# Spectral layer with a mixture of experts on one core: four scatters in flight for the last pair, other PSUM banks for the early jobs, and a new written order

## The chip, the cores and the metric

One core of a Trainium2 chip runs the whole kernel in one launch. The metric is the device time of one execution in microseconds; lower is better. The numbers of an execution differ a little between runs, so the time of a kernel is the median of several.

## The reference, cut to what matters

```python
X  = np.fft.rfft(x, axis=1)                      # x: 8 batches, 1856 positions, 256 channels, float32
Yr = Xr @ w_r - Xi @ w_i + b_r                   # the spectrum goes through a complex 256 x 256 layer
Yi = Xr @ w_i + Xi @ w_r + b_i
Yr = sign(Yr) * max(|Yr| - 0.01, 0)              # soft threshold, the same for Yi
y  = np.fft.irfft(Yr + 1j * Yi, n=1856, axis=1)  # back to 14,848 rows of 256 channels
# routing: one of 4 groups by argmax(y @ w_group), then one of the group's 4 experts; weight = product of both softmax values
h  = max(y[rows of an expert] @ w1[g, e], 0)     # 256 -> 1024
out[rows] = weight * (h @ w2[g, e])              # 1024 -> 256
```

## The kernel before, in words

The eight batches go through in four *pairs*. The transform of 1856 = 29 x 64 positions is made of matmuls. Most products are split into a high and a low part, and three matmuls are added up for one product.

Until about 550 us the kernel follows a written order, the string `ORDER` (lines 58 to 78). Each of its 2040 letters issues one step on one engine, and every engine works through its own steps in that order and never passes over one that waits. Within one letter the steps come by number, so "the 17th s" is the first s of the second pair. These are the letters that matter here.

- TensorE (PE): `c` first transform stage (`a_mm`, line 622), `e` second stage (`f_mm`, 636), `k` the complex layer (`m_mm`, 679, 24 matmuls), `r` first inverse stage (`b_mm`; line 326 for three pairs, 715 for the last), `v` second inverse stage (326), `x` a transpose (`p_turn`, 750), `G` the gate logits (773), `U` and `D` the two matmul layers of an early job (`up_mm` 845, `down_mm` 866 and 867).
- VectorE (DVE): `d` (352), `h` (654), `o` the threshold's sum (692), `q` and `u` low parts (594), `s` the transpose that brings an `r` result into the row tile `v` (`b_turn`, 719), `R` one small step of the routing (185 to 268), `V` low part of an expert's weights (`w_low`, 807), `I`, `T`, `Y`, `B`, `J` steps of an early job (297, 455, 834, 855, 878).
- ScalarE (ACT): `w` (742), `W` high part of an expert's weights (`w_high`, 802), `X` (830), `A` (851), `E` (873), and others.
- SyncE (SP): `l` loads 1 MB (lines 611 for inputs of pairs 2 and 3, 616 for expert weights), `F` fetches the rows of an early job (445 and 452).
- GpSimd (POOL): `S` scatters 128 rows of one pair to the lists of their experts in DRAM (line 277), `K` stores results (543).

A pair has 32 scatters, numbered over all pairs, so S1 is the first of pair 0, S33 of pair 1, S65 of pair 2 and S97 of pair 3. A scatter waits until the one two places ahead of it has landed (`FLY = 2`). Two sets of row tiles `v` are used in turn halves: the first `s` of pair 1 (s17) overwrites rows that S1 to S16 send, the first of pair 2 (s33) rows that S33 to S48 send, and the first of pair 3 (s49) rows that S65 to S80 send. The framework makes each such `s` wait until those scatters have landed.

Four experts have *early jobs* in the ordered phase, two each of 256 rows. A job fetches its rows (`F`), transposes and splits them (`T X Y`), multiplies (`U`), applies the ReLU in two parts (`A B`), multiplies again (`D`), scales (`E J`) and stores (`K`). After the ordered phase comes a late phase that works through the rest of the lists from about 553 us to the end; its code is written out separately and reads the same lists.

[...] `r` of the last pair writes into `pp`, which `U` uses too. `D` writes into `py` for the first two jobs and into `bank()` for the rest.

Of the kernel before, what the change touches and what calls it, by code (L numbers as in the profile page):

```python
# [58 lines left out]
ljeljjcfedghcfgheidikkfnhgimojknZmojenZmcfoeghZjcdfiehgdikkfnhmgojeinkmfoghZZjiknmojZenmcfoeghZjcdfeghikdiknmf  # L59
ojhgeZnmcfoegdjchZikdikfnhmgojeinkmfoghjZZiknmojZenmcfoejdgcfhghcidZkidknmjoZcnmcdjocdpcdpcdppqdZrZqepsrfqehpg  # L60
rsfiehpgskiqqqqemfrghrprsipespsnrjkspqqqrmqorfgsrpkhpspisnjqemqfqrghrprsipesnrjsksqqorfomrhgskinsjotuctmuvtdvw
uctwuvtdvtuwcwuvtdtvuwctuwcutldcfdgxnhxjzeydxuiGyoxxyeyGxvykwtuGmxvfznhkwojtguiemxfvnzhgkjwotiuGmxfHvRyRvwhRvw
RRRtvRRwRxRwxtRxRtezRzyGRRnRGRRugjxReRyRRuivRvwkwuoRmvfRkRwRghnRjRRixmRxzeSfzgGRhnxojSeoyciGSdcHcRlRSdRcRRRRcR
RSRkRRdRRSRRRRRRcmRRdSfklRgnhSjdiRdmeoSfRcRgnRcRjSRcRhkRSRdiddScomfkldgShniojSemnkfSoghjiSemnkfSoghppqSpqemqrp
riSsprpsepSsnkfqghjSqiqjrmoSrsprnspeSspkfogjhSqiqrmqSrsprnsepSspkfogSjhqiqrSfqgrhmsriSnespkspjSqpqqSrfqgrhmsri
SnesrjsescotcdtuctuvtukuwtdudxofvgzhvmwvwixwxzteznuxtoGyuvtGwuvtxjuwkztuxfvgzhmkwintojuxfGgzvhmvwiewxnxtzeoyjG
utvHvwRRvuRwRRvtRwRRRxwRxyuxyGRRyvRtGRRwRRuxtxRyRukyRRRRRvmRGfRgkwRRnRRjRRhSvomxweiSzfxghncziSoeljdGcHSRcRdRcR
RRSRcRRRklRRSdRRRRRRRScRRmRRfkghSndidjcSdmocfdghRSendiRcjRSRclRRcRSdkRRddSocmcSfdghnkldjSoiemSnkfojShgiemSnkfo
# [1181 lines left out]
```

## Time and profile before

| What | Value |
| --- | --- |
| median of 3 runs | 1205.69 us (1204.61 to 1211.43) |
| the profiled execution's own time | 1195.48 us |
| its span in the trace | 1193.6 us |
| mean granted TensorE clock of it | 0.989 of full speed |
| busy: PE, DVE, ACT, POOL | 1149.6, 791.7, 672.9, 261.9 us |

The profiled execution is 10.2 us shorter than the median of the runs, and 1.9 us of its time lie outside the span. Durations below come from that one execution. An engine's idle time is given beside the instruction that ended it, with what released it. Matmuls are pipelined: the start of one to the start of the next tells more than the length of one.

### The profile page before, as it was taken

Reading aid. Unit: us, or ns where it says so; the run is one execution under the profiler, and the core shown is the slowest. Engines: PE = TensorE matmul, PEld = TensorE weight load, DVE = VectorE, ACT = ScalarE, POOL = GpSimd, SP = SyncE. Lnnn points to the kernel's source line nnn. Section 1 sums busy time; section 2 is a strip of 40 time slices with the busy share of each in tenths; the row PEclk is TensorE's granted clock in tenths of the full one; section 3 lists DMA queues with packets and bytes.
Section 4 is the critical chain, followed back from the end, with each engine's and each line's share of the span. In section 5 each row is a group of like instructions: output and inputs, shape, how many; then the busy total and the mean of one; then the engine's idle time right before and its main releaser. Section 6 shows DMA issues by size and latency. Waiting matters only on the chain. (4 is left out here: it accounts for less than half of the span.)

```text
span 1193.6 us, 20882 instructions
## 1 busy us (share of the span) xinstructions
PE 1149.6 (96%) x7428; PEld 990.6 (83%) x7428; DVE 791.7 (66%) x1806; ACT 672.9 (56%) x1506; POOL 261.9 (22%) x257
## 2 busy tenths in 40 slices
PE   8999999999999889998899999999999999999997
PEld 5988889897889569887889888888898898798776
DVE  4449676978787778845785845846767566475542
ACT  2777867685778565534364734634546455454432
POOL 1000013503533532561112111111111111111101
PEclk9999999999999999999999999999999999999989
DMA  9872114103311255443353554454434356455200
GB/s 387 327 279 85 37 34 139 66 1 118 118 38 38 66 135 136 142 145 95 96 177 120 150 202 133 120 230 130 121 113 135 110 174 195 118 177 195 102 10 28
DMA packets 114602, 155.82 MB, mean 131 GB/s; under 512 B 89274, under 2 KB 90045, under 8 KB 104000
## 3 DMA queue, kind: packets, MB, share of 16 engines
q1 hardware_dynamic: 95616, 104.33, 28.7%
q0 software_dynamic: 12048, 30.67, 6.9%
q10 hardware_dynamic: 6832, 19.47, 4.2%
q8 instruction: 59, 0.97, 0.3%
q14 instruction: 47, 0.39, 0.1%
HBM read 104.47 MB, written 52.46 MB: 131 GB/s over the span
## 5 line engine op out<-in xcount | busy, mean ns | idle before, releaser
L556 PE MATMUL py<-big,hh 128*128 128x512 f32 x824 | 289.6, 394 | 0.0
L487 PE MATMUL ph<-xth,big 128*128 128x384 f32 (+1 forms) x896 | 255.5, 361 | 4.0 <-ACT xth L474 3.4
L543 POOL DMA_INDIRECT out_dram<-yo,si x123 | 119.8, 974 | 568.7 <-DVE yo L564 497.2
L557 PE MATMUL py<-big,hl 128*128 128x256 f32 x824 | 230.4, 280 | 2.5 <-DVE hl L493 2.3
L277 POOL DMA_INDIRECT xs_d<-v,sloti x128 | 138.7, 1084 | 338.9 <-ACT xh L649 154.6
L493 DVE SCALAR_TENSOR_TENSOR hl<-ph,hh 128x256 fp32r<-128x256 f32 x448 | 151.7, 380 | 62.0 <-ACT hh L491 59.7
L487 PEld LDWEIGHTS ph<-xth,big 128*128 128x128 f32 x896 | 165.7, 189 | 22.5 <-ACT xth L474 6.2
L556 PEld LDWEIGHTS py<-big,hh 128*128 128x128 f32 x824 | 154.5, 187 | 35.8 <-issue 3.2
L491 ACT ACTIVATE hh<-ph 128x256 fp32r<-128x256 f32 x448 | 133.9, 352 | 78.3 <-PE ph L487 74.7
L487 PE MATMUL ph<-xtl,big 128*128 128x384 f32 (+1 forms) x448 | 162.2, 362 | 2.6 <-DVE xtl L475 2.6
L557 PEld LDWEIGHTS py<-big,hl 128*128 128x128 f32 x824 | 155.5, 189 | 4.0 <-DVE hl L493 2.9
L563 ACT ACTIVATE yo<-py,si 128x256 f32<-128x256 f32 x103 | 48.8, 473 | 151.5 <-PE py L557 146.8
L564 DVE SCALAR_TENSOR_TENSOR yo<-py,si,yo 128x256 f32<-128x256 f32 x103 | 49.5, 482 | 109.5 <-ACT yo L563 108.2
L679 PE MATMUL pw<-wh,xh 128*128 128x256 f32 x480 | 120.2, 292 | 0.0
L432 DVE TENSOR_TENSOR big<-xt,big 128x512 fp32r<-128x512 f32 x168 | 114.1, 682 | 0.0
L679 PE MATMUL pw<-wl,xh 128*128 128x256 f32 x480 | 113.5, 278 | 0.0
L431 ACT CAST big<-xt 128x512 fp32r<-128x512 f32 x168 | 103.7, 621 | 0.0
L487 PEld LDWEIGHTS ph<-xtl,big 128*128 128x128 f32 x448 | 84.6, 189 | 12.8 <-DVE xtl L475 5.3
L679 PEld LDWEIGHTS pw<-wh,xh 128*128 128x128 f32 x480 | 90.8, 189 | 2.8 <-issue 2.4
L679 PEld LDWEIGHTS pw<-wl,xh 128*128 128x128 f32 x480 | 90.7, 189 | 2.6 <-issue 2.4
L692 DVE TENSOR_TENSOR big<-rp,rn 128x512 f32<-128x512 f32 x60 | 42.0, 705 | 45.1 <-ACT rp L686 34.2
L636 PEld LDWEIGHTS pg<-CF,big 128*128 128x128 f32 x480 | 63.8, 198 | 8.5 <-issue 2.7
(200 smaller groups left out, 2034.5 us busy)
## 6 DMA issues: line engine op xcount, KB each, us to landing
xt<-in_w_dram SPq DMA_DIRECT2D x50, 1024.0 KB
xs_d<-zero ACTq DMA_DIRECT2D x16, 1170.0 KB
big<-in_w_dram SPq DMA_DIRECT2D x16, 1024.0 KB
xt<-in_x_dram SPq DMA_DIRECT2D x8, 1024.0 KB
xg<-xs_d SPq DMA_DIRECT2D x64, 96.0 KB
xg<-xs_d SPq DMA_DIRECT2D x48, 128.0 KB
big<-in_x_dram SPq DMA_DIRECT2D x4, 1024.0 KB
v<-in_x_dram SPq DMA_DIRECT2D x4, 1024.0 KB
```

The costliest lines, as they stand in the source:

```text
L277: ins = nc.gpsimd.indirect_dma_start(out=xs_d, out_offset=bass.IndirectOffsetOnAxis(ap=sl_, axis=0), in_=row, in_offset=None, bounds_check ...
L431: nc.scalar.copy(out=wt[:, 2 * i, cs], in_=raws[i][:, cs])
L432: nc.vector.tensor_tensor(out=wt[:, 2 * i + 1, cs], in0=raws[i][:, cs], in1=wt[:, 2 * i, cs].bitcast(F32), op=ALU.subtract)
L487: nc.tensor.matmul(o[:, :n], lhsT=a_[:, ch, fs], rhs=b_[:, ch, 0:n], start=k == 0, stop=k == 5)
L491: nc.scalar.activation(out=hh[:, f, :m], in_=ov, func=AF.Relu)
L493: nc.vector.scalar_tensor_tensor(out=hl[:, f, :m], in0=ov, scalar=0.0, in1=hh[:, f, :m].bitcast(F32), op0=ALU.max, op1=ALU.subtract)
L543: ins = nc.gpsimd.indirect_dma_start(out=out, out_offset=bass.IndirectOffsetOnAxis(ap=ids.si[:, t:t + 1], axis=0), in_=ysb, in_offset=None ...
L556: nc.tensor.matmul(o, lhsT=hh[:, f, ts], rhs=w2b[:, :, f, :], start=f == 0, stop=f == 7, skip_group_check=True)
L557: nc.tensor.matmul(o[:, 0:D], lhsT=hl[:, f, ts], rhs=w2h[:, f, :], start=False, stop=f == 7, skip_group_check=True)
L564: nc.vector.scalar_tensor_tensor(out=ysb, in0=o[:, 0:D], scalar=gate_w, in1=ysb, op0=ALU.mult, op1=ALU.add)
L636: nc.tensor.matmul(o[:, m * 128:(m + 1) * 128], lhsT=zys[pr][:, k, ch * 128:(ch + 1) * 128, bt], rhs=T_v[:, k, :], start=True, stop=True)
L679: nc.tensor.matmul(y[:, bt * D:(bt + 1) * D], lhsT=a_[:, bt * 2 + ch, cs], rhs=w_[:, ri, ch, :], start=False, stop=fin, skip_group_check=True)
```

## The change: what it does

The number of scatters in flight becomes a tuple by pair, two for the first three pairs and four for the last. `r` of the last pair writes into `bank()` instead of `pp`. `D` of all jobs writes into `pg`. `py` goes, and `pp` has three banks, so that eight are in use as before. The result tiles `yp` are five instead of three, the fetch buffers `xg` and `xi` five instead of six. Two small filler tiles shift where a few tiles lie in SBUF.

The order is new from end to end. It has the same number of each letter, except that eight copies go from `z` (DVE) to `y` (ACT). Two of its lines, with the old ones they replace, stand in the diff for all.

```diff
-FLY = 2
+FLY = (2, 2, 2, 4)
...
-XI = {6: 4, 2: 8}
+XI = {5: 4, 2: 8}
...
-jShppqpqeSpqrfqripsSrpqrgqgmeSsnkspjSspqrqSfhrgsirmSsrnsepjSspkpqpqSqrqfhrSpsripqrpqSgeqpskSqssSrfhrgsirSsrses
...
+ocHRcRRdScRRRRdcSRRkdlRSRdRcSmfcdghcRnSdikjdSoRRRRRRRkSmRRfRgShnjoRRmcRSiRncldkjSdoRRSRRcmRSncdjocpdlpSdpqepqS
+qrqfgrhprpqSiepqskSfhgiqsSrnsrSpsrpqrmpqSsjkpqSqsrsnSrpsrpSqrmqpsjepSqfeqgShrfiseghprSiqksSssrSfogrsnSrhkmsWis
...
-            if len(sent) >= FLY:
-                tc.add_manual_dep(ins.ins, sent[-FLY], landed, reason="few scatters are on their way at a time")
+            if len(sent) >= FLY[pr]:
+                tc.add_manual_dep(ins.ins, sent[-FLY[pr]], landed, reason="few scatters are on their way at a time")
...
-            for before in range(1, FLY):
+            for before in range(1, min(FLY[pr], len(sent))):
...
     def h_pair(pool, nf):
+        if pool not in shifted:
+            pool.tile([128, 16], F32, name="aside", bufs=1)
...
-            psum["b", pr, j] = o = early["pp"].tile([128, 512], F32, name="ph")
+            psum["b", pr, j] = o = bank()
...
-        xgs[n] = load_rows(early["mp"], slice(e * CAP + j * LEV, e * CAP + j * LEV + LEV), LEV, 6)
+        xgs[n] = load_rows(early["mp"], slice(e * CAP + j * LEV, e * CAP + j * LEV + LEV), LEV, 5)
...
-        apart(early["mp"], 16)
...
-            psum["d", n, t] = early["py"].tile([128, 512], F32, name="py") if n < 2 else bank()
+            psum["d", n, t] = pg.tile([128, 512], F32, name="pg")
...
-                yp.append(ph.enter_context(tc.tile_pool(name="yp", bufs=3)))
+                apart(early["mp"], 8)
+                yp.append(ph.enter_context(tc.tile_pool(name="yp", bufs=5)))
...
-                early["pp"] = ph.enter_context(tc.tile_pool(name="pp", bufs=2, space=PSUM))
-                early["py"] = ph.enter_context(tc.tile_pool(name="py", bufs=1, space=PSUM))
+                early["pp"] = ph.enter_context(tc.tile_pool(name="pp", bufs=3, space=PSUM))
```

Line numbers of the changed kernel are up to two higher than those of before (`b_turn` is line 721 there, `w_low` 809).

The first place is SP's queue around the first row fetches. `L616` (`L618` after) loads 1 MB of expert weights, `L445` and `L452` fetch the ids `xi` and the rows `xg` of one job. Before:

```order
11 L611 DMA xt<-in_x_dram 128x2048 x8
12 L616 DMA xt<-in_w_dram 128x2048 x2
13 L445 DMA xi<-xs_d 128x2x2
14 L452 DMA xg<-xs_d 32x8x64 x4
15 L616 DMA xt<-in_w_dram 128x2048
16 L445 DMA xi<-xs_d 128x2x2
17 L452 DMA xg<-xs_d 32x8x64
18 L616 DMA xt<-in_w_dram 128x2048
19 L452 DMA xg<-xs_d 32x8x64 x3
```

After:

```order
11 L613 DMA xt<-in_x_dram 128x2048 x8
12 L618 DMA xt<-in_w_dram 128x2048 x4
13 L445 DMA xi<-xs_d 128x2x2
14 L452 DMA xg<-xs_d 32x8x64 x4
15 L445 DMA xi<-xs_d 128x2x2
16 L452 DMA xg<-xs_d 32x8x64 x4
```

The third and fourth weight load stand ahead of the first fetch now, and no weight load stands among the first fetches.

The second place is PE's queue at the first inverse stage of the last pair, `r49` to `r64` (`L715`, `L717` after), and the first job's first layer `U` (`L845`, `L846` after). Before:

```order
1676 L679 MATMUL pw<-wh,xl 128x256 x8
1677 L715 MATMUL ph<-big,CI 128x512 x16
1678 L845 MATMUL ph<-xth,big 128x256
1679 L845 MATMUL ph<-xtl,big 128x256
1680 L845 MATMUL ph<-xth,big 128x256 x2
```

After:

```order
1666 L681 MATMUL pw<-wh,xl 128x256 x8
1667 L717 MATMUL bank<-big,CI 128x512 x7
1668 L846 MATMUL ph<-xth,big 128x256
1669 L846 MATMUL ph<-xtl,big 128x256
1670 L846 MATMUL ph<-xth,big 128x256 x2
1671 L846 MATMUL ph<-xtl,big 128x256
1672 L846 MATMUL ph<-xth,big 128x256 x2
1673 L846 MATMUL ph<-xtl,big 128x256
1674 L846 MATMUL ph<-xth,big 128x256 x2
1675 L846 MATMUL ph<-xtl,big 128x256
1676 L846 MATMUL ph<-xth,big 128x256
1677 L717 MATMUL bank<-big,CI 128x512 x9
```

One `U` of the first job stands after seven of the sixteen `r`, and the `r` write into `bank` tiles.

The third place is DVE's queue ahead of s33, the first transpose of pair 2 (`L719`, `L721` after). `L268` ends a routing, `L692` (`L694`) is the threshold's sum, `L654` (`L656`) a low part of the second stage, `L594` (`L596`) the low part that the `r` needs. Before:

```order
294 L268 TENSOR_TENSOR base<-base,inc 128x16
295 L352 STREAM_TRANSPOSE big<-bank 128x16x16x2 x2
296 L692 TENSOR_TENSOR big<-rp,rn 128x512
297 L352 STREAM_TRANSPOSE big<-bank 128x16x16x2
298 L654 TENSOR_TENSOR xl<-pg,xh 128x4x128
299 L352 STREAM_TRANSPOSE big<-bank 128x16x16x2
300 L692 TENSOR_TENSOR big<-rp,rn 128x512 x2
301 L654 TENSOR_TENSOR xl<-pg,xh 128x4x128
302 L692 TENSOR_TENSOR big<-rp,rn 128x512
303 L654 TENSOR_TENSOR xl<-pg,xh 128x4x128
304 L594 TENSOR_TENSOR sl<-big,sh 128x512 x4
305 L719 STREAM_TRANSPOSE v<-bank 128x16x32
```

After:

```order
276 L268 TENSOR_TENSOR base<-base,inc 128x16
277 L352 STREAM_TRANSPOSE big<-bank 128x16x16x2
278 L694 TENSOR_TENSOR big<-rp,rn 128x512
279 L352 STREAM_TRANSPOSE big<-bank 128x16x16x2 x2
280 L596 TENSOR_TENSOR sl<-big,sh 128x512 x4
281 L656 TENSOR_TENSOR xl<-pg,xh 128x4x128
282 L596 TENSOR_TENSOR sl<-big,sh 128x512 x2
283 L721 STREAM_TRANSPOSE v<-bank 128x16x32
```

The transpose stands nearer to the routing: one threshold step instead of four and one `L656` instead of three are left between them. In the string, the stretch from S33 to s33 holds six `k`, six `e`, two `r`, two `x`, one `v` and one `G` of PE's large steps before, and four `k`, four `e`, three `r`, three `x` and two `G` after; thirteen `c` and four `l` stand in it in both. From S1 to s17 three `l` stand before, and none after. From S65 to s49 there is no `l` in either.

## Rows read from the trace of the kernel before

**Rows 1.** The page's span and busy times, with their share of the span and the number of instructions.

```profile
span 1193.6 us, 20882 instructions
...
PE   1149.6 (96%) x7428; PEld 990.6 (83%) x7428; DVE 791.7 (66%) x1806; ACT 672.9 (56%) x1506; POOL 261.9 (22%) x257
```

**Rows 2.** The view by windows: the window's start and end, its length, then the busy time of each engine in it (with the number of instructions), the granted TensorE clock, the share of the DMA engines and GB/s.

```profile
0.00:100.00 100.00, 96.64 (x637) 78.55 (x638) 51.30 (x81) 59.20 (x112) 3.31 (x6) 1.00 0.81 321
...
200.00:210.00 10.00, 9.19 (x69) 8.51 (x67) 5.92 (x8) 7.63 (x15) 5.18 (x6) 1.00 0.18 63
210.00:220.00 10.00, 8.96 (x47) 7.88 (x48) 9.58 (x15) 6.76 (x14) 6.81 (x5) 0.83 0.17 61
...
310.00:320.00 10.00, 8.67 (x63) 7.86 (x62) 8.55 (x13) 8.20 (x17) 5.96 (x6) 1.00 0.20 72
...
440.00:450.00 10.00, 6.93 (x52) 5.79 (x52) 6.34 (x15) 6.69 (x13) 0.00 (x0) 0.83 0.85 180
...
490.00:500.00 10.00, 8.35 (x64) 7.61 (x63) 8.55 (x26) 3.42 (x7) 5.02 (x6) 1.00 0.58 190
...
530.00:540.00 10.00, 5.90 (x43) 5.27 (x44) 3.23 (x5) 2.77 (x5) 6.08 (x7) 1.00 0.24 87
```

**Rows 3.** The timeline of POOL, DVE and PE around s17: start, length, engine, line, operation, tiles, and in brackets the idle time before it and what ended it. S1 starts at 170.78 and S16 at 203.81.

```profile
170.78 1.12 POOL L277 DMA_INDIRECT xs_d<-v,sloti  x1 [149.79 <-ACT xh L649]
...
187.47 1.14 POOL L277 DMA_INDIRECT xs_d<-v,sloti  x1 [3.52 <-DMA xs_d<-v,sloti]
...
203.81 0.97 POOL L277 DMA_INDIRECT xs_d<-v,sloti  x1 [0.30 <-issue]
...
207.29 2.05 DVE L719 STREAM_TRANSPOSE v<-bank 128x512 f32<-128x512 f32 x2 [4.04 <-DMA xs_d<-v,sloti]
...
210.81 0.50 PE L326 MATMUL bank<-sl,tph 128*128 128x512 f32 x1 [1.62 <-DVE sl L594]
```

**Rows 4.** The timeline of POOL and DVE from S33 (276.98) and S48 (312.06) to s33, and SP's weight loads of that stretch.

```profile
276.98 1.40 POOL L277 DMA_INDIRECT xs_d<-v,sloti  x1 [40.05 <-DVE xl L654]
...
288.39 0.97 POOL L277 DMA_INDIRECT xs_d<-v,sloti  x1 [5.19 <-DMA xs_d<-v,sloti]
...
312.06 1.10 POOL L277 DMA_INDIRECT xs_d<-v,sloti  x1 [0.30 <-issue]
...
314.77 1.09 DVE L719 STREAM_TRANSPOSE v<-bank 128x512 f32<-128x512 f32 x1 [1.25 <-PE bank L326]
...
280.14 5.54 SPq L611 DMA_DIRECT2D xt<-in_x_dram  x2
295.43 6.50 SPq L616 DMA_DIRECT2D xt<-in_w_dram  x2
```

**Rows 5.** The timeline of POOL where no load is under way: two scatters of the last pair, with one scatter between them that is not shown.

```profile
411.90 0.97 POOL L277 DMA_INDIRECT xs_d<-v,sloti  x1 [1.04 <-DMA xs_d<-v,sloti]
...
415.10 1.08 POOL L277 DMA_INDIRECT xs_d<-v,sloti  x1 [0.95 <-DMA xs_d<-v,sloti]
```

**Rows 6.** The timeline of PE: one `e` (line 636, to the next start) and one `k` (line 679, from its first matmul to the next step's).

```profile
293.33 1.11 PE L636 MATMUL pg<-CF,big 128*128 128x128 f32 x8
294.27 0.27 PE L247 MATMUL bank<-oh,ones 128*128 128x256 bf16 x1
...
296.56 0.68 PE L679 MATMUL pw<-wh,xh 128*128 128x256 f32 x1
...
299.70 0.59 PE L622 MATMUL bank<-xt,cA 128*128 128x512 f32 x1
```

**Rows 7.** The timeline of PE and DVE in the last pair's first inverse stage.

```profile
411.54 2.04 PE L715 MATMUL ph<-big,CI 128*128 128x512 f32 x4 [0.37 <-DVE v L719]
413.96 2.03 PE L715 MATMUL ph<-big,CI 128*128 128x512 f32 x4 [0.39 <-DVE v L719]
...
423.66 0.35 PE L845 MATMUL ph<-xth,big 128*128 128x256 f32 x1 [0.43 <-issue]
...
414.64 0.69 DVE L807 TENSOR_TENSOR big<-xt,big 128x512 fp32r<-128x512 f32 x1
415.24 1.99 DVE L719 STREAM_TRANSPOSE v<-ph 128x512 f32<-128x512 f32 x2
```

**Rows 8.** The timeline of SP, ACT, DVE and PE around 440 us.

```profile
436.56 1.50 SPq L616 DMA_DIRECT2D xt<-in_w_dram  x1
...
443.10 0.62 ACT L802 CAST big<-xt 128x512 fp32r<-128x512 f32 x1 [3.91 <-DMA xt<-in_w_dram]
...
444.54 0.17 DVE L297 TENSOR_SCALAR si<-xi 128x2 int32<-128x2 f32 x1 [3.66 <-DMA xi<-xs_d]
...
444.78 1.44 PE L750 MATMUL bank<-K,v 128*128 128x128 f32 x6 [2.95 <-ACT v L742]
```

**Rows 9.** The timeline of PE and ACT at the end of the ordered phase.

```profile
531.41 0.38 PE L845 MATMUL ph<-xth,big 128*128 128x256 f32 x1 [1.50 <-DVE hl L855]
538.68 0.39 PE L845 MATMUL ph<-xth,big 128*128 128x256 f32 x1 [2.61 <-issue]
...
529.33 0.62 ACT L830 CAST xth<-sl 128x512 fp32r<-128x512 f32 x1 [5.29 <-PE bank L867]
...
537.30 0.60 ACT L851 ACTIVATE hh<-ph 128x512 fp32r<-128x512 f32 x1 [3.18 <-PE bank L866]
...
553.71 0.44 PE L487 MATMUL ph<-xth,big 128*128 128x384 f32 x1 [2.80 <-ACT xth L474]
```

More of the change, by code (lines that the diff above doesn't have):

```diff
@@ L58 @@
 ORDER = """
[L59 to L68, printed above, removed]
@@ L74 @@
[L74 to L77 removed]
+jlcjljcdcdcdcdcdedcfehgdcfcidgedchcidedkknfghmjeoncfcidgmhkZjdioZenkfghmjoieZnfkghmjoieZnfkghmjoieZfmkhnijogZe
@@ new lines @@
+fmkhnijogZkfmhniojemncfocjdcggdZkZdhiemnkfojZhgienkmfjoZhgienkmfjoZhgienkmfjoZhgienkmfjohgZienemfjkohgZZpiqpqp
+rfrqnhrgisemskpjqpspqprqqfrnrhgsmeijsrpespqkpqpqqsrforhgrnisemsrpjqkpspqpqrqfrsghkpiqssrforhnrisemscgjscdctdct
+otcndldctdmcdjcdeldkoouuucnucfdcmhgicdjdcldcdcdcdvldvwovwxwxeyyxtvyuGwvtxwkuyttutuxuvnfzGvwhtixwkuytmugjoxvnze
+fwhvmixjoGykwttuguxvfyGnhviHewRRwRxmRRxRRvyRRyGRwvRjRxRowkRRRyRRtRRRtRRtGgfeunuRvumRkhgwiRRjRRRRvRfvSowhewSixx
+nykymSgjoSGfenhxmSixzjkzSogeSfGnShkmHiRRjRoSgRRRRReRfSRknRRhmRjRoSgRieRRRSfRRRknRRmhgjSoieSfRpRhpkqpSqpqgiSqne
@@ new lines @@
+RfRRkgRnRmRRhmSjojrofSrsprpqrpqSsgepiSsrnskmpjsSqqSqrfghrsprpSqepqriSsnkpsmsSjqrSfqghrsprpeSspisrSksqqSqrfhSgr
+sirskSshStioutctuvdtvwuutcwuvtvdnwuvwovwxwxyxyxyGyxnGyxetyuctfGugvdthetwuviutxmeuwzjxovtykuwtnumxmojGjvzHfvgov
+wRwRkhwttutuxiuRxfvyRhyGwRvRRiRgRvwReRwRvRnReRRRnwRxRRRkRmRyjomjoGRfRxgRnkRyRmRjRRSRxhxmoyeSzixfGgyhcnSedijlSG
+ocHRcRRdScRRRRdcSRRkdlRSRdRcSmfcdghcRnSdikjdSoRRRRRRRkSmRRfRgShnjoRRmcRSiRncldkjSdoRRSRRcmRSncdjocpdlpSdpqepqS
+qrqfgrhprpqSiepqskSfhgiqsSrnsrSpsrpqrmpqSsjkpqSqsrsnSrpsrpSqrmqpsjepSqfeqgShrfiseghprSiqksSssrSfogrsnSrhkmsWis
@@ new lines @@
+jWoWtkotututunvunVvwVtvVwvwutxwvzWxuwWxVvyzlWVewGVtfxxtuhyeizGfuxghgvykiwttutuxWGWuzvmVvVmwelowxmoxyeyGfnhvjov
+iwkHwRRjRjRRRgRtRRxxfRyRkRhyRmRRRRiRnRRRGgRomkRnjottuRvtumuReRwnRxRfeRyRvgRfRhGgShwviioxSweztxjuejuySvGwSvxwky
+SSxmkznSfoghSjiGefgHRSkmRRhnRRRiSRRjRReRfRgSkoRhmRRiSRRnRRRRRkjRSfghmSonRioRkmRSnRRRRSRRomnSoFSrsrSsrSsrITrsrS
+XYrSsUsrsSABrSsrsrsSrsSrsrsSrsrSsUsWWVtSUAVtuSBUttuvAuAvuwSvBwBSvwtxwxDuttzuvtuvyuFwGwvtFvwuDwITtFDtuXtuvYWFTv
+WwtuDwVFtuvVWxwuUFtVWzWxVAlxWVUByVyGAUlIIIIEIEBFUJAKJBxKAxXzDByYGuxxUyyIGAxxBUyHyRGRRARvRRRRvwRtRDwRRRuxxERRRR
@@ L78 @@
+DyRRyRRGRRDJBRvKWTRWUwRRWxRWRAURWRRBWSWvAzVDwSXBGWVxSEVJvySYDwVSlVxEUVJySVGAVSUlHBSRUARTRBSURRRRRSRDRXRSRRYDAR
+ARSBUBSERRRRJUARSRBUARRSBUSTRDTKXTRKYDRRKRURERRRDSJDASABSDEBAJUSWBWVWVUSWVASVWUBWWSVWVDXSVYDEVSJUSAABDSBUESAJS
+UBABSUSDXSYDKUEJKDKDAAKBDBAKEBUJKUABUDDEJKDAABDBEJDKDEJDKEJK
 """
```

8 lines of the change are left out of this document (removed).

## The prediction

> **What bounds the kernel now.** I read the page's busy times first: TensorE (PE) is busy for 1149.6 of 1193.6 us [rows 1], 44 us short of the span, so nothing the change does on another engine counts unless it ends a wait of PE. The number of PE's steps doesn't change. The second view is the one by windows, to find where PE is idle or slow [rows 2]. In the first 100 us it lacks 3.4 us, from 200 to 220 us 0.81 + 1.04 us, from 310 to 320 us 1.33 us, from 440 to 450 us 3.07 us, from 490 to 500 us 1.65 us and from 530 to 540 us 4.10 us. In two of these windows the granted clock is 0.83, so the work that is done there is slower too. The third view is the timeline of each place: who ended the wait. It names four causes.
>
> At s17, VectorE (DVE) waits 4.04 us until the sixteen first scatters have landed, and PE then waits 1.62 us for DVE [rows 3]. Around 440 us ScalarE (ACT) waits 3.91 us for a weight load that was issued at 436.56 and used at 443.10, behind it stands the copy that PE waits 2.95 us for, and DVE waits 3.66 us for a row fetch of the same queue [rows 8]. In the last pair's first inverse stage PE waits 0.37 to 0.39 us for DVE in every two steps `r` [rows 7]. At the end of the ordered phase PE waits 1.50 and 2.61 us for hidden layers of the early jobs [rows 9].
>
> The step from the ordered to the late phase, where PE waits 2.80 us for the first rows [rows 9], ends in the same letters before and after (`EJK`), so I leave it as it is.
>
> **The change part by part.** The sum is made against the profiled execution's own 1195.48 us. That execution is 10.2 us below the median of the runs shown, so I add the sum to 1205.7.
>
> *Start.* The first steps `c` of the second pair move ahead of `e`, where PE has something to do while DVE finishes. All of the window's loss is 3.4 us [rows 2], most of it before the first data. Two input loads are issued nearer to their use, about 6 us of PE work; the load of rows 8 took 6.5 us from issue to use, so up to 1 us could be lost. Ends -2 and +1, I take **-1**.
>
> *s17.* Sixteen scatters took from 170.78 to about 207.3, 36.5 us [rows 3]. Where no load is under way, two scatters take 411.90 to 415.10, 3.2 us [rows 5], so that sixteen take 8 x 3.2 = 26 us and some 2 us to land. The rest are waits like the 3.52 us before 187.47, beside input loads. The new order has no load between S1 and s17, and the stretch is about as long as before less 3 us, so the scatters are in time. What goes is 1.85 us of idle PE and the lower clock of 210 to 220 us, 0.17 x 8.96 = 1.5 us. Ends 0 (they are late for another reason) and -4, I take **-3.4**.
>
> *s33.* Here the change goes the other way. S33 started at 276.98 and s33 at 314.77, 37.8 us later [rows 4]. The row names PE as the one that ended the last 1.25 us, but S48 left at 312.06 and needs about as long to land, so both came together: the stretch fitted the scatters just about. It was long because four 1 MB loads lie in it. The first two are issued from 280.14 on, the pair of scatters beside them holds up the next until 288.39, 5.19 us of waiting [rows 4]. Against 26 + 2 us undisturbed, each load costs (37.8 - 28) / 4 = 2.5 us. The new order keeps the four loads and takes two `k` and two `e` out of the stretch. A `k` is 299.70 - 296.56 = 3.1 us and an `e` 294.27 - 293.33 = 0.94 us [rows 6], together 8.1 us. An `r`, an `x` and a `G` come in and a `v` goes out; none is longer than an `e` and a half, which I take as 1.5 us. So s33 stands 6.6 us earlier and waits 1.25 + 6.6, some 8 us, for the scatters. All `s` of pair 2 and their low parts queue behind it on DVE, and PE needs them: its next `r` lacks a bank. One `k` (3.1 us) stands in front of that and hides a part. Left are 5 us; a granted clock of 0.83 over 10 us, as after s17, would add 1.5. Ends 0 and +9.5, I take **+5**.
>
> The rows show the pair beside a load ending with the load. [...]
>
> *s49.* No load lies between S65 and s49, before or after. The new stretch is some 3.6 us of PE steps shorter, about 26 us, and sixteen undisturbed scatters take 26 to 28 [rows 5]. Ends 0 and +2, I take **+0.7**.
>
> *First inverse stage of the last pair.* It is bound by DVE: four matmuls follow four after 413.96 - 411.54 = 2.42 us, in which DVE does two `s` and one other step, while PE has 2.04 us of matmuls [rows 7]. The `V` (0.6 us each, 415.24 - 414.64) of the first weights are done earlier in the new order, and a `U` goes in between, which came at 423.66. Five `V` are 3 us of DVE; part comes back in the forward phase of that pair, where DVE and PE have about the same to do. The three banks for `r` instead of two change nothing as long as DVE is the slower. Ends -4 and 0, I take **-2**.
>
> *Around 440 us.* All four weight loads of the first two experts now stand ahead of the first row fetch in SP's queue, and the waits of rows 8 go with their cause: 3.07 us of idle PE and 0.17 x 6.93 = 1.2 us of clock, 4.3 us [rows 2]. Next late is the second row fetch: it reads rows of the second list part, so SP holds all later fetches until S96 has landed. That was 3.66 us of DVE in the row; here I take 1 us of PE. Ends -4.3 and +1, I take **-3.3**.
>
> *Early jobs.* 1.65 + 4.10 us are idle in the two late windows [rows 2]. The ACT steps at 529.33 and 537.30 waited 5.29 and 3.18 us and name matmuls of `D` as what ended it, though by the code neither needs a `D`, but a `U` [rows 9]. I can't say what held them. The new order leaves more steps between a `U`, its `A` and `B`, and the `D` that needs them; three banks of `pp`, two of `pg` and five result tiles give `U` and `D` room. A wait of 4 us on ACT would then be half hidden. `D` in `pg` competes with nothing there, because `e` is done by then. Ends -5.7 and 0, I take **-4**.
>
> *Four in flight.* The last scatters land before the last job is done, before as after, so their end bounds nothing. Four scatters may hold up a row fetch that passes them. I cost it at 0, ends -1 and +1. The tiles moved in SBUF and the eight copies from DVE to ACT (0.6 us each, hidden where neither is the bound) are 0 too.
>
> The sum: -1 - 3.4 + 5 + 0.7 - 2 - 3.3 - 4 = -8.0 us, so 1195.5 would become 1187.5 and the median 1205.7 becomes **1197.7 us**.
>
> **The rivals.**
>
> *No net gain, about 1205.* The late answers of ACT at the end of the ordered phase come from no step of the order, so they turn up again at other steps, and s33 costs its full 8 us: -3.4 + 8 + 0.7 - 2 - 3.3 = 0, so 1205.7. For it: the total work of PE, ACT and DVE is the same, so a new order can only win waits, and these are 15.4 us of idle PE in the windows of rows 2, and 2.7 of clock. Against it: two of the named waits lose their cause, whatever becomes of the rest.
>
> *Slower, about 1213.* One mechanism: the scatters of pair 1 beside the four loads. s33 waits 8 us, DVE falls behind in the stretch that it bounds, the one `k` doesn't hide any, since it was needed for DVE's own input, and the clock stays at 0.83 for 20 us (3 us): +11. What the other places win must then shrink to 4 us, of the 14 forecast, as it would if the fetches held by S96 bring back the wait at 440 us and the job waits recur. +11 - 4 = +7, 1213. It decides from a wait of about 8 us at s33 on. For it: the load count in the stretch is the same and its length isn't. Against it: in the rows each of the stretch's loads was issued when a tile came free, so that a later one may slip behind s33.
>
> *A larger gain, about 1189.* The scatters at s33 land in time because one or two of the loads slip, so the 5 us fall away, and the start and the jobs give all they have: -2 - 3.4 - 3 - 3.3 - 5 = -17.
>
> *The change does not do what it says.* Four in flight do nothing for the end, as reckoned above; that is part of the forecast, not another time.
>
> **How the numbers follow.** The forecast (1193 to 1202) has 45%, no net gain (1201 to 1210) 30%, slower 15%, the larger gain 10%. A measurement of this kernel can tell about 0.5%, 6 us, from no change, so faster means below 1199.7 and slower above 1211.7. Faster: 0.8 of the forecast and all of the larger gain, 46%. Slower: the slower case and the upper edge of no net gain, 17%. The rest, 37%, is the same. For 8 in 10 the range takes in most of the larger gain and the start of the slower case, 1188 to 1212; the forecast's own is 1193 to 1202.
>
> **What would show it.** In the changed kernel's profile, no DVE wait above 1 us at the first `s` of pair 1 and a granted clock of 1.00 after it; a DVE wait of 5 to 8 us for a scatter at the first `s` of pair 2, and PE short by 3 to 6 us there; no wait of ACT for a weight load after the first row fetches; less than 3 us of idle PE in the last 30 us before the late phase. The forecast is wrong if s33 is in time (then too high), or if the job waits come back as long as before (then too low). The late phase must be as long as before within 1 us; if it isn't, the time comes from something that I have not seen.

## The result, and the profile after

The changed kernel takes 1214.93 us (median of 9 runs, 1213.04 to 1219.72); before took 1205.69 us (1201.91 to 1211.43, 9 runs). The ratio is 1.0075 with a 95% interval of 1.0053 to 1.0097: slower, by the 0.5% that the prediction set, and above both the forecast's own range (1193 to 1202) and the whole one (1188 to 1212).

One warning on the two traces. That of before shows an execution of 1195.48 us, shorter than each of its nine timed runs; the one after shows 1215.43 us, like its median. Side by side they differ by 20 us where the medians differ by 9, so about half of what the two show as a loss belongs to those two executions and not to the kernels.

The page of the changed kernel, its first lines and the first line on DMA issues:

```profile
span 1213.5 us, 20920 instructions
...
PE 1159.1 (96%) x7428; PEld 1000.3 (82%) x7428; DVE 789.8 (65%) x1798; ACT 674.8 (56%) x1514; POOL 257.2 (21%) x257
...
xt<-in_w_dram SPq DMA_DIRECT2D x50, 1024.0 KB
```

PE has as many matmuls as before [rows 1] and is busy for 9.5 us more, at a mean granted clock of 0.979 instead of 0.989. The last line should end in the time from issue to landing and does not; that will matter. Next the windows of rows 2 and four more (PE, PEld, DVE, ACT, POOL busy, granted clock, DMA share, GB/s):

```profile
0.00:100.00 100.00, 97.79 (x642) 79.78 (x643) 48.88 (x77) 58.24 (x113) 3.31 (x6) 1.00 0.80 317
210.00:220.00 10.00, 9.65 (x60) 8.41 (x59) 10.00 (x15) 8.02 (x16) 6.71 (x6) 1.00 0.17 62
310.00:320.00 10.00, 4.63 (x20) 3.34 (x19) 5.17 (x7) 1.99 (x5) 6.27 (x7) 0.82 0.22 77
440.00:450.00 10.00, 5.28 (x29) 4.68 (x28) 4.07 (x9) 4.07 (x9) 0.00 (x0) 0.80 0.52 80
490.00:500.00 10.00, 7.53 (x64) 6.72 (x56) 5.42 (x15) 1.09 (x3) 7.59 (x8) 1.00 0.66 246
500.00:510.00 10.00, 6.92 (x33) 6.30 (x34) 3.52 (x11) 2.92 (x7) 5.08 (x6) 0.66 0.21 72
502.00:506.00 4.00, 3.61 (x14) 3.02 (x15) 1.44 (x4) 0.60 (x1) 2.90 (x3) 0.50 0.26 91
530.00:540.00 10.00, 7.69 (x37) 7.01 (x38) 4.24 (x7) 3.38 (x7) 5.63 (x7) 0.66 0.54 185
540.00:550.00 10.00, 5.82 (x39) 4.92 (x37) 1.55 (x3) 1.25 (x3) 5.36 (x6) 0.92 0.24 77
```

The window of s17 (210 to 220) is nearly full. PE lacks 5.37 us at s33 (310 to 320), 4.72 us around 440, and, what was not expected, 2.5, 3.1, 2.3 and 4.2 us in four windows of the early jobs, half of them at a low clock: from 502 to 506 us the chip granted 0.50, after PE had done nothing for 4.26 us.

DVE's timeline at s17, at s33 and around 440 us, against rows 3, 4 and 8:

```profile
211.27 1.10 DVE L721 STREAM_TRANSPOSE v<-bank 128x512 f32<-128x512 f32 x1
...
314.83 1.08 DVE L721 STREAM_TRANSPOSE v<-bank 128x512 f32<-128x512 f32 x1 [6.08 <-DMA xs_d<-v,sloti]
...
443.24 0.17 DVE L297 TENSOR_SCALAR si<-xi 128x2 int32<-128x2 f32 x1 [4.41 <-DMA xi<-xs_d]
446.13 0.71 DVE L455 STREAM_TRANSPOSE sl<-xg 128x512 f32<-128x512 f32 x1 [2.65 <-DMA xg<-xs_d]
```

The s17 wait is gone (no bracket). s33 waits 6.08 us for the scatters, where some 8 had been worked out. Around 440 us the weight load no longer holds ACT, but the row fetch of the second list part, behind S96, holds DVE for 4.41 + 2.65 us, and PE for 4.72 us.

The rest is in the early jobs. PE and ACT of the changed kernel at 494 to 502 us, and the two last waits before the late phase:

```profile
494.45 0.28 PE L846 MATMUL ph<-xth,big 128*128 128x256 f32 x1
...
497.25 0.28 PE L868 MATMUL pg<-big,hl 128*128 128x256 f32 x1
501.79 0.58 PE L846 MATMUL ph<-xth,big 128*128 128x256 f32 x1 [4.26 <-ACT xth L831]
...
549.17 0.58 PE L846 MATMUL ph<-xth,big 128*128 128x256 f32 x1 [4.03 <-ACT xth L831]
...
574.85 0.44 PE L487 MATMUL ph<-xth,big 128*128 128x384 f32 x1 [2.81 <-ACT xth L474]
```

```profile
501.12 0.62 ACT L831 CAST xth<-sl 128x512 fp32r<-128x512 f32 x1 [8.02 <-issue]
503.95 0.60 ACT L852 ACTIVATE hh<-ph 128x512 fp32r<-128x512 f32 x1 [2.05 <-remote]
...
531.50 0.62 ACT L831 CAST xth<-sl 128x512 fp32r<-128x512 f32 x1 [3.88 <-remote]
...
548.50 0.62 ACT L831 CAST xth<-sl 128x512 fp32r<-128x512 f32 x1 [8.24 <-remote]
```

The cast `X` at 501.12 may overwrite `xth` as soon as the `U` that reads it is done. The last matmul of that `U` ended at 494.73. ACT waits 8.02 us all the same, and the view names nothing that ended it ("issue"; "remote" is no better). A trace also records when an engine raises a semaphore. TensorE's signal for that matmul stands there at 501.06, 6.32 us after the recorded end, and ACT starts 0.06 us behind it. I call this a *late answer*. Some records of signals are missing in this trace, so a signal is matched with its matmul by the step that needs it and starts right behind it. Six of this trace, each of which ended a wait of ACT:

```
matmul ended   signal    lag
494.73         501.06     6.32
495.31         503.92     8.61
496.01         506.82    10.81
497.53         509.03    11.50
525.63         531.48     5.85
542.34         548.47     6.13
```

The first late matmul starts at 574.85 instead of 553.71 [rows 9]; from there to the end it takes 638.6 us, before 639.9, which is 1.3 us where the prediction allowed 1. All of the loss lies in the ordered phase. The profiled execution of before has late answers too: 3.59 us at 529.30, 5.11 at 533.63, 4.22 at 537.28. The ACT steps of rows 9 start 0.03 us after the first and 0.02 us after the third. They are what the prediction could not explain. The recorded ends of matmuls are modelled, so the traces do not tell whether the matmul or only its signal was late; the waiting engine is held either way.

### The profile page after: what moved, and what is told of

Its sections match the earlier page's. It is cut to its first block, busy times and chain, and to the rows that moved or that the text cites. A ratio compares the mean times of both kernels' runs of the same rounds, so it can differ in the third digit from the quotient of the medians.

```text
span 1213.5 us, 20920 instructions
## 1 busy us (share of the span) xinstructions
PE 1159.1 (96%) x7428; PEld 1000.3 (82%) x7428; DVE 789.8 (65%) x1798; ACT 674.8 (56%) x1514; POOL 257.2 (21%) x257
## 5 line engine op out<-in xcount | busy, mean ns | idle before, releaser
L277 POOL DMA_INDIRECT xs_d<-v,sloti x128 | 133.7, 1045 | 338.2 <-DVE big L694 161.3
L721 DVE STREAM_TRANSPOSE v<-bank 128x512 f32<-128x512 f32 x64 | 64.8, 1094 | 9.2 <-DMA xs_d<-v,sloti 6.1
L846 PE MATMUL ph<-xth,big 128*128 128x256 f32 x256 | 54.6, 304 | 13.9 <-ACT xth L831 8.3
```

Source lines behind the costliest of these rows:

```text
L277: ins = nc.gpsimd.indirect_dma_start(out=xs_d, out_offset=bass.IndirectOffsetOnAxis(ap=sl_, axis=0), in_=row, in_offset=None, bounds_check ...
L721: nc.vector.transpose(out=vs[pr][:, :, :, j * 16:(j + 1) * 16].rearrange("p h r d -> p d h r"), in_=psum.pop(("b", pr, j)).rearrange("p (k ...
L846: nc.tensor.matmul(o[:, i * 256:(i + 1) * 256], lhsT=a_[:, ch, fs], rhs=b_[:, ch, :], start=k == 0, stop=k == 5)
```

## The experiments

All eighteen, with the measured ratio to before (95% interval), the medians, and where the first late matmul starts in the one trace. "Gaps" are traces without landing times, in which semaphore records are missing; in "whole" ones they are there.

| Kernel | Ratio to before | Median / before, us | Records | Late phase from, us |
| --- | --- | --- | --- | --- |
| after (first measurement) | 1.0075 [1.0053, 1.0097] | 1214.93 / 1205.69 | gaps | 574.85 |
| e1 after, two in flight | 1.0055 [1.0027, 1.0082] | 1206.01 / 1201.26 | gaps | 561.91 |
| e10 the same | 1.0039 [1.0010, 1.0069] | 1205.15 / 1201.84 | gaps | 558.04 |
| e2 after, four also in pair 1 | 1.0094 [1.0059, 1.0129] | 1211.10 / 1201.26 | gaps | 577.56 |
| e9 the same | 1.0054 [1.0013, 1.0096] | 1208.12 / 1201.84 | gaps | 562.13 |
| e3 after with the old order | 1.0207 [1.0155, 1.0259] | 1226.42 / 1201.26 | gaps | 587.24 |
| e16 that, two in flight | 1.0031 [1.0009, 1.0053] | 1197.70 / 1193.95 | whole | 557.24 |
| e4 before, four in flight | 1.0072 [1.0042, 1.0102] | 1210.33 / 1201.26 | gaps | 572.94 |
| e11 the same | 1.0063 [1.0029, 1.0096] | 1208.52 / 1201.84 | gaps | 569.73 |
| e5 e1, stores counted | 1.0060 [1.0039, 1.0081] | 1197.68 / 1191.33 | whole | 558.57 |
| e6 before, stores counted | 0.9998 [0.9967, 1.0030] | 1190.11 / 1191.33 | whole | 552.28 |
| e7 after with pauses | 1.0232 [1.0191, 1.0273] | 1218.31 / 1191.33 | whole | 576.95 |
| e8 after again | 0.9977 [0.9957, 0.9996] | 1187.88 / 1191.33 | whole | 547.24 |
| e14 after again | 0.9965 [0.9945, 0.9984] | 1189.59 / 1193.95 | whole | 548.82 |
| e15 before again | 0.9997 [0.9976, 1.0018] | 1192.64 / 1193.95 | whole | 552.42 |
| e12 after, two loads held | 1.0037 [1.0000, 1.0073] | 1204.67 / 1201.84 | gaps | 564.56 |
| e17 the same | 1.0055 [1.0029, 1.0082] | 1209.73 / 1203.06 | gaps | 557.53 |
| e13 e12, two in flight | 1.0016 [1.0001, 1.0030] | 1194.99 / 1193.95 | whole | 554.91 |
| e18 e12, three in flight | 0.9975 [0.9947, 1.0004] | 1198.62 / 1203.06 | gaps | 556.01 |

The runs came in five groups, each on one chip with its own runs of before: e1 to e4, e5 to e8, e9 to e12, e13 to e16, e17 and e18. All traces of a group are alike in their records.

### Is it the four in flight? (e1 to e4)

e1 takes them back, e2 gives them to pair 1 too, e3 keeps all of the change but the order, e4 adds them alone to before.

```diff
# e1
-FLY = (2, 2, 2, 4)
+FLY = (2, 2, 2, 2)
# e2
-FLY = (2, 2, 2, 4)
+FLY = (2, 4, 2, 4)
# e4, from before
-FLY = 2
+FLY = (2, 2, 2, 4)
```

> The changed kernel with two scatters in flight for the last pair too, as before the change. Theory A (four scatters in flight beside weight loads are what holds up PE's and ACT's answers in the stretch of the early jobs, where the changed kernel lost some 17 us against the kernel before): the three long ACT waits at X5, X7 and X8 (8.0, 3.9, 8.2 us) shrink to under 3 us and the time falls to about 1205. Rival B (the new order and pools cost it, whatever the scatters do): the waits stay, 1212 to 1217. In both the wait of s33 stays at about 6 us.

> The changed kernel with four scatters in flight for pair 1 as well. Theory: s33 waits 6.1 us because each pair of scatters beside a 1 MB load ends with the load; with four in flight only every fourth is held, S33 to S48 take 6 us less, the wait of s33 falls under 2 us, PE gets back 5 to 8 us there, about 1208. Rival (DMA shares are what limits, or the scatters are held by POOL's own pace): s33 waits 4 us or more and the time is 1213 to 1216.

> Everything of the change but the order: the order of the kernel before with four scatters in flight for the last pair, the new banks and the new buffer counts. If the order is what costs, the time is that of the kernel before, 1203 to 1207. If the four scatters or the banks cost it, 1210 or more. The wait of s33 is 1 to 2 us as before in any case.

> The kernel before with only the four scatters in flight for the last pair. Theory A (the four scatters slow the early jobs): 1210 or more. Rival B (they do nothing, since the last scatters land before the last job is done): within 2 us of the kernel before, 1204 to 1208.

e4 is slower by 0.72% with nothing else changed, nearly as much as the whole change. In its trace the late answers reach 5.7 us at 488 and 10.8 us at 544. In e1 there is none above 1 us until 532.87 (then 2.45, 11.08 at 544.28 and 6.3 at 551.62), and the late phase starts 12.9 us earlier than in the first trace of after. e2 moves them: with four in flight in pair 1 they turn up at 323 to 330 us (2.5 to 5 us), where the other traces of this group and the first two have none above 1 us, and again from 505 on (up to 12.9). The wait at s33 is gone in e2, as its theory asked, but the time does not fall. So there are more late answers, and at more places, with more scatters on their way; two in flight do not end them. e3 shows that the old order with the new banks is no way out: 14.05 us of lag at 494.13, 17.59 at 498.38, and PE idle for 15.1 us in one piece. By its medians e1 is still not faster than before, so four in flight is not all of it.

### Dense stores, pauses, and a second condition (e5 to e8)

Late answers stand where GpSimd issues scatters and stores back to back (POOL's steps 0.30 us apart). Of the six above four end while it sends, and two in a pause of it (509.03 in one of 3.00 us, 548.47 in one of 3.63). In the first trace of after:

```profile
497.95 0.97 POOL L277 DMA_INDIRECT xs_d<-v,sloti  x1 [0.30 <-issue]
499.23 0.97 POOL L277 DMA_INDIRECT xs_d<-v,sloti  x1 [0.30 <-issue]
```

e5 and e6 let a store count as one of the two in flight; e7 makes GpSimd rest behind every second scatter of the last pair; e8 is the changed kernel again.

```diff
# e5 (from e1) and e6 (from before)
+    def in_turn(ins):
+        if len(flown) >= 2:
+            tc.add_manual_dep(ins.ins, flown[-2], landed, reason="few scatters and stores are on their way at a time")
+        flown.append(ins.ins.name)
...
+            in_turn(ins)
...
-        store(units.pop(("y", n, t)), ids[n], t, "out")
+        in_turn(store(units.pop(("y", n, t)), ids[n], t, "out"))
# e7, from after; also four result tiles yp instead of five
+            if pr == NP - 1 and len(sent) % 2 == 0:
+                rest_t = rt.tile([128, 320], F32, name="rest", bufs=1)
+                for _ in range(4):
+                    m = nc.gpsimd.memset(rest_t, 0.0)
...
```

> The changed kernel with two in flight for the last pair, and with the early jobs' stores counted in that rule too, so that GpSimd can never send more than two scatters or stores in a row without waiting for one to land. Theory: TensorE's answers are late (up to 11 us) while GpSimd sends one indirect DMA right behind the other, and come when it pauses; with a pause after every two the late answers fall under 2 us and the ordered phase ends 10 us earlier than in the run with two in flight alone, some 1195 where the kernel before has 1201. Rival (late answers come from the weight loads or from the number of DMAs under way): one of over 5 us is left behind the last scatters and the time is that of the run with two in flight, +0.3 to +0.7% of the kernel before.

> The kernel before with stores and scatters under one rule of two in flight. Theory: its late answers of 3.6 to 5.1 us at 526 to 540 us go, and the time falls by 3 to 6 us. Rival: they stay, within 2 us of the kernel before. If the stores' wait holds up the last scatters, the late phase's first fetch is late and 2 to 4 us are lost there.

> The changed kernel, four in flight for the last pair, with four memsets on GpSimd (some 1.3 us, to a tile that nobody reads) behind every second scatter of that pair, and four result tiles instead of five to make room. Theory (back-to-back sending is what holds TensorE's answers up, not the number under way): late answers fall under 2 us in the stretch of the early jobs, as with two in flight, and the time is 3 to 10 us below that of the changed kernel. Rival (the number under way counts, or any work of GpSimd): they stay at 6 us and more and the time is that of the changed kernel or above.

> The changed kernel again, for a comparison on the same chip with the runs beside it: +0.5 to +1.0% against the kernel before, late answers of 6 us and more at three places of the early jobs.

These tested little of what they were made for, because in this group no answer is late: the largest lag of any signal of TensorE is 0.05 us, in all four kernels. e8, the changed kernel itself, is now 0.23% *faster* than before. What differs in the records can be read on the page. The line of the weight loads in e14, a later run of the changed kernel of the same sort:

```profile
span 1187.8 us, 20920 instructions
...
xt<-in_w_dram SPq DMA_DIRECT2D x50, 1024.0 KB, 5.2
```

The landing time is there, and the trace holds 9,816 semaphore updates of DMAs instead of 7,608 and 977 instead of 935 of TensorE for the same program. Records of ScalarE (1335 instead of 1254) and VectorE (1364 instead of 1265) are missing as well, but signals of these two engines are never late: no recorded one stands more than 0.04 us behind its step, in any trace. The groups without such times all have late answers, the two groups with them none, and before is 7 to 15 us shorter in these (1191 and 1194 against 1201 to 1206 us). It is not the chip: the first two groups ran on the same one, some 20 minutes apart. e7 only shows a price: with pauses the last scatters come late, and the first late matmul waits.

```profile
576.95 0.69 PE L496 MATMUL ph<-xth,big 128*128 128x384 f32 x1 [30.65 <-ACT xth L483]
```

e5 costs 0.6%: its late phase begins 11.3 us after that of e8, and its last `D` waits 5.5 us for DVE. e6 is the same as before.

### Repeats, and the loads at s33 (e9 to e12)

e9, e10 and e11 are e2, e1 and e4 again, to see which answer holds. e12 tests the sum's largest loss: of the four loads in the stretch from S33 to s33, two of inputs and two of weights, the two of weights wait until S48 has landed (one `l` also moves behind the 48th `S` of the order).

```diff
+                ins = nc.sync.dma_start(out=t, in_=src[e * 128:e * 128 + 128])
+                if e == 0:
+                    tc.add_manual_dep(ins.ins, sent[47], landed, reason="behind the scatters that s33 needs")
```

> The changed kernel with four scatters in flight for pair 1 too, run again. Theory: runs with TensorE answers that are late and with records missing, and runs without either, are two conditions of the chip's recording, and only in the first do four scatters in flight cost anything. Without late answers, s33 waits under 2 us instead of 6.1 and the time is 4 to 6 us below the changed kernel's (0.995 of the kernel before or lower). With them, as in the first run of it, +0.7% or more. Rival (four in flight delay TensorE in any condition): +0.5% or more and late answers, whatever the records show.

> The changed kernel with two scatters in flight for the last pair, run again. Without late answers: within 0.2% of the changed kernel's 0.998, as the last scatters land before the last job is done in both. With late answers: some 0.2 to 0.6% above the kernel before.

> The kernel before with four scatters in flight for the last pair, run again. Without late answers: within 0.2% of the kernel before. With them: +0.5 to +0.9%, as in its first run.

> The changed kernel, with the first two weight loads held until S48 has landed, so that only two of the four loads lie between S33 and s33. Theory (each load costs its pair of scatters 2.5 us): the wait of s33 falls from 6 us to 1 to 2, and the time by 3 to 6 us against the changed kernel (0.994 of the kernel before without late answers, 1.003 with them). Rival (the loads are not what holds the scatters): the wait stays at 5 us or more and the time that of the changed kernel. If the loads come too late for the first W, an ACT wait for a weight load of over 1 us shows at W1.

e11 repeats e4 (+0.63% and +0.72%), e10 repeats e1 (+0.39% and +0.55%). e9 stays below the 0.7% expected for it (+0.54%, where e2 had +0.94%; the intervals overlap). The group has gaps and late answers again. s33 in e12, then SP's two held loads behind the last input loads:

```profile
311.78 1.08 DVE L723 STREAM_TRANSPOSE v<-bank 128x512 f32<-128x512 f32 x1 [2.41 <-DMA xs_d<-v,sloti]
```

```profile
281.09 5.47 SPq L613 DMA_DIRECT2D xt<-in_x_dram  x2
...
311.72 0.83 SPq L618 DMA_DIRECT2D xt<-in_w_dram  x2
```

Two loads fewer, and the wait at s33 falls from 6.08 to 2.41 us; two loads are left. In e9, with the four loads and four scatters in flight, it falls to nothing:

```profile
310.31 1.13 DVE L721 STREAM_TRANSPOSE v<-bank 128x512 f32<-128x512 f32 x1
```

So the scatters were late through the loads (e12), as long as only two of them may be on their way (e9). S33 and S48 on POOL, in the first trace of after, then in e12 and in e9:

```profile
277.15 1.38 POOL L277 DMA_INDIRECT xs_d<-v,sloti  x1 [38.52 <-DVE xl L656]
...
312.15 0.97 POOL L277 DMA_INDIRECT xs_d<-v,sloti  x1 [0.45 <-DMA xs_d<-v,sloti]
```

```profile
277.78 1.38 POOL L277 DMA_INDIRECT xs_d<-v,sloti  x1 [39.14 <-DVE xl L658]
...
308.73 1.50 POOL L277 DMA_INDIRECT xs_d<-v,sloti  x1 [0.30 <-issue]
```

```profile
277.55 1.37 POOL L277 DMA_INDIRECT xs_d<-v,sloti  x1 [36.74 <-DVE xl L656]
...
300.68 0.97 POOL L277 DMA_INDIRECT xs_d<-v,sloti  x1 [0.30 <-issue]
```

From S33 to the first `s` of pair 2 it takes 314.83 - 277.15 = 37.7 us with four loads and 311.78 - 277.78 = 34.0 us with two; against the undisturbed 28 us of the prediction that is (37.7 - 28) / 4 = 2.4 and (34.0 - 28) / 2 = 3 us for a load, and 1.85 us for each of the two that e12 took away. In the trace of e14 S35, S37 and S45 land at 286.46, 291.83 and 309.92, 0.27 to 0.41 us behind a load that lands at 286.19, 291.44 and 309.51. S45 takes 5.29 us from issue to landing beside its load, and S47 takes 2.38 without one: 2.9 us more, within the 2.4 to 3 us worked out for a load. What makes a scatter land right behind the load was not shown. In e9 S48 leaves 23.1 us after S33, at about the time at which the weight loads are issued (299.72). It pays for its gain with late answers of 3 to 5 us at 326 to 329.

### The same questions with whole records (e13 to e16), and a compromise (e17, e18)

e13 is e12 with two in flight, e14 and e15 are after and before again, e16 is e3 with two in flight, e17 is e12 again, and e18 is e12 with `FLY = (2, 2, 2, 3)`.

> The changed kernel with both repairs: two scatters in flight for the last pair, and the first two weight loads held until S48 has landed. The two gains lie at different places and should add up. With late answers: 1.0039 less the 4.5 us that the held loads won (0.4%), 0.998 to 1.002 of the kernel before. Without them: 0.993 to 0.996. Rival: what the held loads win before 400 us is lost again behind it, the time is that of two in flight alone.

> The changed kernel beside the others on one chip. If records of semaphore updates are missing in this run, late answers of 6 us and more and +0.5 to +1.0%; if none is missing, no late answers and 0.996 to 1.000 of the kernel before.

> The kernel before, for a trace under the condition of this chip. With records missing: late answers of 3 to 6 us in the stretch of the early jobs, and an ordered phase of 551 to 565 us. Without: none above 0.5 us, and the ordered phase ends at 545 us or earlier. Ratio 1.00.

> The order of the kernel before with the new banks and buffer counts and two in flight throughout. The same with four in flight was +2.1%, the kernel before with four alone +0.7%. If the new banks cost by themselves (D in two banks that the order was not written for), +1% or more is left; if only together with four in flight, within 0.4% of the kernel before.

> The changed kernel with only the first two weight loads held until S48 has landed, four in flight for the last pair, run again. The held loads won 3.2 us at s33 beside two in flight, and the last scatters of the changed kernel leave at 536.6, early enough for an ordered phase that ends at 542. Without late answers: the changed kernel's 0.9965 less 0.3%, 0.992 to 0.995 of the kernel before, the best of all. With late answers: 1.001 to 1.006, as in its first run. Rival: the late phase's first matmul waits more than the 2.8 us of before, and the 3.2 us are lost there.

> The same with three scatters in flight for the last pair. Without late answers: the last scatters leave at about 540, the late phase's first matmul waits up to 7 us, 0.994 to 0.999. With late answers: GpSimd pauses after every third, the answers are late by less than with four, 0.998 to 1.004.

e14 against e15 is the comparison the prediction meant to make, with whole records on both sides. Windows of e14:

```profile
210.00:220.00 10.00, 9.66 (x63) 8.52 (x63) 9.92 (x16) 8.05 (x17) 6.17 (x5) 1.00 0.14 50
310.00:320.00 10.00, 5.91 (x26) 4.56 (x26) 5.51 (x7) 2.38 (x5) 5.84 (x6) 0.79 0.18 66
440.00:450.00 10.00, 5.83 (x28) 5.08 (x28) 5.18 (x11) 4.47 (x10) 0.00 (x0) 0.77 0.51 83
490.00:500.00 10.00, 10.00 (x81) 9.66 (x80) 9.62 (x31) 4.28 (x9) 6.92 (x8) 1.00 0.58 213
500.00:510.00 10.00, 10.00 (x68) 9.00 (x67) 8.03 (x16) 3.71 (x8) 7.85 (x8) 1.00 0.30 101
530.00:540.00 10.00, 10.00 (x72) 9.28 (x71) 4.03 (x7) 3.28 (x6) 7.71 (x8) 1.00 0.29 100
```

And of e15:

```profile
310.00:320.00 10.00, 8.07 (x59) 7.25 (x58) 7.98 (x12) 7.72 (x16) 6.45 (x6) 1.00 0.23 82
440.00:450.00 10.00, 6.34 (x45) 4.93 (x44) 5.35 (x13) 6.74 (x13) 0.00 (x0) 0.76 0.82 175
500.00:510.00 10.00, 8.04 (x54) 6.88 (x53) 3.38 (x7) 2.61 (x6) 5.84 (x6) 1.00 0.18 66
530.00:540.00 10.00, 10.00 (x73) 9.32 (x72) 3.82 (x6) 3.46 (x6) 7.22 (x8) 1.00 0.24 89
```

The losses at s33 and around 440 us are there in e14, the holes in the jobs are not. The cast `X` that waited 8.02 us in the first trace waits here for a `U` that it needs, and POOL sends just as densely at that moment:

```profile
493.15 0.62 ACT L831 CAST xth<-sl 128x512 fp32r<-128x512 f32 x1 [2.13 <-PE ph L846]
```

```profile
492.56 1.01 POOL L277 DMA_INDIRECT xs_d<-v,sloti  x1 [0.30 <-issue]
493.88 0.97 POOL L277 DMA_INDIRECT xs_d<-v,sloti  x1 [0.30 <-issue]
...
536.55 0.97 POOL L277 DMA_INDIRECT xs_d<-v,sloti  x1 [0.30 <-issue]
```

Dense sending alone, then, makes no late answers; it takes the other condition too. e13 shows what four in flight is good for, and that the two repairs do not add up as expected (+0.16%). Its ordered phase is 3.9 us shorter than e14's, since s33 waits less, and yet its late phase begins 6.1 us later: the last scatter leaves at 545.09 instead of 536.55, the first late rows come late, and PE waits for them.

```profile
554.91 0.69 PE L487 MATMUL ph<-xth,big 128*128 128x384 f32 x1 [12.82 <-ACT xth L474]
```

e10, with two in flight in the new order, waits 9.89 us there; e14 waits 2.81. In e1, the same kernel as e10, late answers keep the jobs going until 559.0, and the wait is 2.88. Two in flight became too few because the new order starts the last pair's scatters later: S97 leaves at 481.55 in e14 and at 465.04 in e15. e16, the old order with the new banks, loses 0.31%; a `D` waits 3.49 us there for DVE to empty a `pg`. The banks gain nothing without the order made for them.

e18 and e17 differ in one digit and ran in one group: 1198.62 against 1209.73 us. The trace of e17 is its fastest execution, 13 us below its median, so the two traces do not show that difference. With gaps, three in flight still has late answers (up to 4.7 us at 515, 7.9 at 542) and sends the last scatter by 536.76. In e18 PE itself stops, too:

```profile
538.73 0.28 PE L848 MATMUL ph<-xtl,big 128*128 128x256 f32 x1 [1.74 <-issue]
...
540.88 0.48 PE L869 MATMUL pg<-big,hh 128*128 128x512 f32 x1 [1.13 <-issue]
542.29 0.28 PE L870 MATMUL pg<-big,hl 128*128 128x256 f32 x1 [0.93 <-issue]
```

None of the three waits for a semaphore, and ScalarE and VectorE do nothing from 532.7 to 542.3 us: TensorE itself stands still, and not only its signals are held up. Such pauses, over 0.3 us ahead of a matmul that waits for no semaphore, come to 0.9 to 6.6 us in eight of the twelve traces with gaps (between 100 and 600 us), and there is none in the eight whole ones.

e18 is the best kernel measured in such a group, at 0.9975 with an interval that just reaches 1; it was not run in a group with whole records, so that it beats both kernels in both conditions is not shown.

## Why the prediction was wrong

Where a kernel's order differs, I compare at equal PE work: the time at which the steps begun so far add up to the same sum of PE durations. After minus before, in the pair of traces with whole records (e14, e15) and in the pair of the first measurement (the terms leave out a few tenths between the places, and hold to about 1 us, as the orders differ). The traces with gaps lie 20 us apart and the medians 9, so some 11 of the +21.1 belong to the two executions:

| Term | Forecast, us | Whole records | With gaps |
| --- | --- | --- | --- |
| start | -1 | +0.4 | up to s33 together -4.0 |
| s17 | -3.4 | -2.1 | |
| s33 (and s49) | +5.7 | +6.5 | +8.9 |
| last pair's first inverse stage | -2 | -4.6 | -4.8 |
| around 440 us | -3.3 | 0 | +2 |
| early jobs | -4 | -3.7 | +19 |
| sum | -8.0 | -3.6 | +21.1 |

- *s17* was right: 0 us of waiting and a clock of 1.00. 2.1 us came of it, not 3.4.
- *s33* was right in place and cause, and near in size: "some 8 us" of waiting "for the scatters" became 6.08 (5.07 in e14), and e12 shows the loads as the cause.
- *The first inverse stage* was right in sign and too small: -4.6, just beyond the end of -4.
- *Around 440 us* failed at the step "here I take 1 us of PE". The cause of rows 8 went as said, but the fetch held by S96, which the step named as next late, is not cheaper than what it replaced: DVE waits 4.41 + 2.65 us, and PE 4.72 us in the window against 3.07 before. In the windows of e14 and e15 PE is busy for 5.83 and 6.34 us, so nothing was won there.
- *Early jobs* failed under the condition that was measured. The step "A wait of 4 us on ACT would then be half hidden" took the late ACT steps of rows 9 for a delay of fixed size that more steps in between could cover. They were late answers, and there are more and longer ones with four in flight: 6 to 11.5 us against 4 to 5. That is no mis-sized term but a mechanism that I had in two rows and did not follow. With whole records the term came out at -3.7, but not by that step, as neither trace has late answers: of e15's 4.2 us of idle PE in the jobs 1.96 end when DVE empties a bank for `D` and 1.82 when DVE has done a `B`, and e14 has none. The other ground of the term, room for `U` and `D` and more steps between them, fits that.
- *Four in flight* failed at "I cost it at 0, ends -1 and +1". With gaps it alone costs before 0.63 to 0.72%, some 8 us; without it the new order's PE waits 9.89 us (e10) and 12.82 us (e13) for the first late rows instead of 2.8. "The last scatters land before the last job is done, before as after" holds for after only because there are four. The step left out both sides: what four do to TensorE's answers, and that the new order starts the last pair's scatters 16.5 us later.

The rival "no net gain" named this mechanism ("come from no step of the order, so they turn up again at other steps") with 30% and put its price at the old size. "Slower" gave the right time by the wrong way: not the clock at s33, but the recurring waits made it. In two of three groups with the changed kernel, e8 and e14, the change is worth -0.23% and -0.35%, both "the same" by the 0.5% of the prediction and well short of the 8 us forecast (the medians lie 3.5 and 4.4 us apart); by the same 0.5% the first measurement is slower. Both are what this kernel does, in conditions that no edit here chooses.

Open: what makes the condition. Records missing and answers late come together by group (12 traces have both, 8 neither), which does not show that one makes the other, and an execution without any recording was not tried. That late answers grow with the scatters in flight is shown as a fact (up to 10.8 us in e4 against 5.11 in before, up to 12.9 in e2 against 11.50 in after, and in e1 none above 1 us until 532.87), not as a mechanism. Before with four in flight was not run in a group with whole records, so that four in flight cost nothing there is seen in the changed kernel alone.

## What to carry to other kernels

When a wait's releaser in the profile has long been done, or the view names none, look up the engine's own signal before you put a price on the wait; a delay with no owner in the order can grow with the change. Take apart from each other a gain for the work that follows and a load on the machine: here the same four scatters in flight save a wait of some 10 us ahead of the late phase (12.82 us in e13 against 2.81 in e14) and come with later answers of TensorE (up to 10.8 us in e4 against 5.11 in before), and in a group with gaps three were the better number (beside the two held loads, e18 against e17). And measure more than one group of runs: by groups, the same edit came out at +0.75% and at -0.35%.
